# Router logits in four column strips out of one turned tile, with a wait ahead of a unit's transposes

## The chip, the cores and the metric

One core of a Trainium2 chip runs the whole program in one launch. The metric is the device time of that launch in microseconds (us), lower is better. The core has a matrix engine (TensorE, "PE"; its weight loads are the rows "PEld"), VectorE ("DVE"), ScalarE ("ACT"), GpSimd ("POOL") and SyncE ("SP"), which here only issues DMA transfers. Each engine takes its instructions in order and waits on semaphores of the others.

## The reference

The input x has 8 sequences of 2880 rows of 192 numbers, all float32. First a causal convolution: with weight (8 heads x 7 taps) turned by a softmax into seven shares per head, every row becomes the weighted sum of itself and the six rows before it, head by head (24 numbers a head).

The 23040 smoothed rows then go through a mixture of experts with two levels of choice:

```
g_logits = x @ w_group                      # 192 x 4
g_idx    = argmax(g_logits);  g_w = softmax(g_logits)[g_idx]
e_logits = x @ w_expert[g_idx]              # 192 x 4
e_idx    = argmax(e_logits);  e_w = softmax(e_logits)[e_idx]
out      = g_w * e_w * (relu(x @ w1[g_idx, e_idx]) @ w2[g_idx, e_idx])
```

w1 is 192 x 1024 and w2 1024 x 192 for each of 16 experts. Each row is worked on by one expert only.

## The kernel before, in words

**Routing.** The rows are cut into 192 blocks of 120, and the blocks into 18 units: the first six have 4, 8, 12, 8, 8 and 8 blocks, the other twelve 12. A unit is a Python generator, `unit` (line 397), whose `yield`s cut it into turns; `step` (line 1087) gives one turn to each of the two or three units alive, in a circle. A unit's turns are, in order: eight convolution turns (lines 437 to 456, one head each: a matmul with a band matrix and an eviction into the unit's tile `xc`, which has three buffers); the transposes of its smoothed rows, four blocks at a time ("a quarter"), columns 0 to 127 in `turn_a` and columns 128 to 191 in `turn_b`, two blocks' narrow columns side by side; the router's logits, `logits` and `logits_back`; softmax and choice on VectorE; the DMA of the smoothed rows to DRAM (`xcd`, line 569, issued by ScalarE); and the lists of rows for each expert, written to DRAM by an indirect DMA (line 644).

**The logits.** The router has 20 outputs, padded to 32 columns. `logits` puts the result of quarter q on partitions 32q to 32q + 31 of one PSUM bank. A quarter has 4 x 120 = 480 rows, so the matmul on the wide part is 480 columns long; the narrow part needs two more of 240 columns, one for the even and one for the odd blocks, with router weights that have zeros in the other half (`wrb`). A unit of 12 blocks thus fills three strips of 32 partitions, one of 8 blocks two, and one of 4 blocks one. ScalarE evicts the bank, `logits_back` transposes the result back so that rows lie on partitions, in four pieces, and ScalarE evicts again. The turned rows are in the tiles `ta` and `tb` with three buffers each, one for every quarter.

**Experts.** Each visit to an expert takes slots of 256 rows: the rows are gathered from `xcd` (line 716), turned (line 738), multiplied by w1 (`hidden`, line 808), evicted with ReLU by ScalarE and VectorE, multiplied by w2 (`back`, line 827), scaled and scattered to the output (line 887). Products are made of float32r pieces, a high and a low part of each operand, so weights are first split (line 674). Once all units are routed, slots are taken in pairs of 512 columns (`hidden_pair`, line 779); a pair's three operands come from `pair_room` (line 769): the high part from the tile `xa`, the low part from `lts`, and the narrow part from `ta`. At the end a tail of 18 smaller slots uses weights that the table `tab` names; every second one loads its weights into the then unused buffers `xin` and `xc` (line 654).

**What sets the order.** The first five units are routed by steps alone, then 100 more steps are taken, and then every expert slot advances the routing by a rate that spreads the remaining turns (line 1225). The program text gives each instruction a priority; a planner then orders each engine's instructions by priority and by costs it assumes, and gives out buffers of a pool as they come free. A few instructions are held in the order of the program. A unit of 12 blocks has 47 turns; from the ninth unit on, one starts when the unit before it has had 23.

Of the kernel before, what the change touches and what calls it, by code (L numbers as in the profile page):

```python
# [9 lines left out]
F32 = mybir.dt.float32  # L10
F32R = mybir.dt.float32r
BF16 = mybir.dt.bfloat16
F16 = mybir.dt.float16
I32 = mybir.dt.int32
U32 = mybir.dt.uint32
AF = mybir.ActivationFunctionType
# [4 lines left out]
P = 128  # L21
BT = 120
UB = 12
QB = 4
# [7 lines left out]
NTAB = 128  # L32
# [4 lines left out]
def conv_moe_kernel(  # L37
# [10 lines left out]
    nc = tc.nc  # L48
# [30 lines left out]
    NL = G + E  # L79
# [13 lines left out]
    for b in range(B):  # L93
        k = b * NB
# [78 lines left out]
    const = ctx.enter_context(tc.tile_pool(name="const", bufs=1))  # L173
    dram = ctx.enter_context(tc.tile_pool(name="dram", bufs=1, space=bass.MemoryType.DRAM))
    pa = ctx.enter_context(tc.tile_pool(name="pa", bufs=1))
    XCB = 2
    pa2 = ctx.enter_context(tc.tile_pool(name="pa2", bufs=XCB))
# [13 lines left out]
    XE = XW + D2  # L191
# [57 lines left out]
    NC = 32  # L249
    wr = const.tile([P, 2, NC], F32, name="wr")  # L250
    nc.vector.memset(wr, 0.0)
    wev = w_expert.rearrange("g d e -> d g e")
    for q, (p0, r0, n) in enumerate(((0, 0, P), (0, P, D2), (D2, P, D2))):
        c = min(q, 1)
# [4 lines left out]
    ident = const.tile([P, P], F32, name="ident")  # L259
# [8 lines left out]
    def clear_table():  # L268
# [12 lines left out]
        out=tri, in_=ones, pattern=[[1, P]], compare_op=ALU.is_gt, fill=0.0, base=0, channel_multiplier=-1,  # L281
# [12 lines left out]
    for nb in sorted({n for _, n in units}):  # L294
# [35 lines left out]
        out=sel, in_=ident.rearrange("p (e l) -> p e l", e=E), axis=AX.X, op=ALU.add)  # L330
    nc.gpsimd.iota(io[:, 0:1], pattern=[[0, 1]], base=0, channel_multiplier=1)
    nc.vector.tensor_scalar(
        out=io[:, 1:2], in0=io[:, 0:1], scalar1=LE - 1, scalar2=None, op0=ALU.bitwise_and)
# [6 lines left out]
    for g in range(NSK):  # L340
        nc.sync.dma_start(
            out=skew[0:R, g * HG:(g + 1) * HG],
            in_=bass.AP(wvd.tensor, wvd.offset + VL - KS - (BT - 1) + g * HG * VL, [[1, R], [VL, HG], [1, VW]]),
# [6 lines left out]
    for v in (3, 4):  # L350
        n = units[v][1]
# [12 lines left out]
    band = const.tile([P, H, BT], F32, name="band")  # L364
    for h in range(H):
        nc.scalar.activation(
            out=band[0:R, h], in_=skew[0:R, h, BT - 1::-1], func=AF.Exp, bias=wm[0:R, h:h + 1],
# [2 lines left out]


    QS = UB // QB
    wrb = const.tile([P, 2, NC], F32, name="wrb")

    def router_weights():
# [9 lines left out]
    for i in range(NXG):  # L385
        t = const.tile([P, XE + XW], F32, name=f"xg{i}")
# [10 lines left out]
    def unit(u, pre=None):  # L397
        c0, nb = units[u]
# [57 lines left out]
                nc.scalar.activation(out=xo, in_=pv, func=AF.Copy)  # L456
        nc.scalar.activation(out=xc[0:BT, 0:nb:2, XW:XE], in_=xc[0:BT, 1:nb:2, 1 + P:XW], func=AF.Copy)
        lg = rt.tile([P, UB, NL], F32, name="lg")[:, 0:nb]
        QN = QB * BT
        NQ = nb // QB  # L460
        parts = {}

        def turn_a(q):
            psa = bank("t")
            for i in range(QB):
                nc.tensor.transpose(psa[:, i * BT:(i + 1) * BT], xc[0:BT, q * QB + i, 1:1 + P], ident[0:BT, 0:BT])
            ta = pa.tile([P, 512], F32, name="ta", bufs=QS)[:, 0:QN]
            nc.scalar.activation(out=ta, in_=psa[:, 0:QN], func=AF.Copy)
            parts[q] = (ta,)

        def turn_b(q):
            psb = bank("t")
            tb = pa.tile([P, QN // 2], F32, name="tb", bufs=QS)
            for i in range(QB // 2):
                k = q * QB + 2 * i
                nc.tensor.transpose(psb[:, i * BT:(i + 1) * BT], xc[0:BT, k, 1 + P:XE], ident[0:BT, 0:BT])
            nc.scalar.activation(out=tb, in_=psb[:, 0:QN // 2], func=AF.Copy)
            parts[q] += (tb,)

        turned_logits = []  # L480

        def logits():
            lgp = bank("l")
            half = QB // 2
            for step in range(3):
                for q in range(NQ):
                    ta, tb = parts[q]
                    o = lgp[q * NC:(q + 1) * NC, 0:QN]
                    if step == 0:
                        nc.tensor.matmul(out=o, lhsT=wr[:, 0], rhs=ta, start=True, stop=False)  # L490
                    else:
                        j = step - 1
                        nc.tensor.matmul(
                            out=o.rearrange("p (i j t) -> p i j t", i=half, j=2)[:, :, j], lhsT=wrb[:, j],
                            rhs=tb.rearrange("p (i t) -> p i t", i=half), start=False, stop=j == 1)
            lgt = pa.tile([P, 512], F32, name="lts", bufs=2)
            nc.scalar.activation(out=lgt[0:NQ * NC, 0:QN], in_=lgp[0:NQ * NC, 0:QN], func=AF.Copy)
            turned_logits.append(lgt)

        def logits_back():  # L500
            lgt = turned_logits.pop()
            w = NQ * NC
            back = bank("l")
            for i in range(QB):
                nc.tensor.transpose(back[0:BT, i * w:(i + 1) * w], lgt[0:w, i * BT:(i + 1) * BT], ident[0:w, 0:w])
            nc.scalar.activation(
                out=lg[0:BT].rearrange("p (q i) n -> p i q n", i=QB),
                in_=back[0:BT, 0:QB * w].rearrange("p (i q n) -> p i q n", i=QB, n=NC)[:, :, :, 0:NL], func=AF.Copy)

        ga, gl, rest = gaps(u)  # L510
        events = {}
# [86 lines left out]
        for b0 in range(0, nb, HB2):  # L598
            n = min(HB2, nb - b0)
# [169 lines left out]
    def pair_room():  # L769
        hi = ff.tile([P, 2, SLOT], F32R, name="xa").rearrange("p a b -> p (a b)")  # L770
        lo = pa.tile([P, 512], F32, name="lts", bufs=2).bitcast(F32R)
        xb = pa.tile([P, 512], F32, name="ta", bufs=QS).bitcast(F32R)
        return hi, lo, xb

    def turn_half(X, k, xs):
# [153 lines left out]
    def table(first=None, nbig=NBIG, nsmall=NSMALL):  # L929
# [115 lines left out]
            return  # L1045
        nc.sync.dma_start(out=tabd, in_=enti)
        yield
        tabt = const.tile([1, NTAB, 4], I32, name="tab")
        nc.sync.dma_start(out=tabt, in_=tabd.unsqueeze(0))
        yield tabt  # L1050

# [434 lines left out]
```

## Time and profile before

| | us |
|---|---|
| median of 3 runs | 1137.57 |
| lowest and highest | 1131.44, 1137.88 |
| profiled execution | 1133.71 |
| its span in the trace | 1131.9 |

| engine | busy us | share of the span |
|---|---|---|
| TensorE, matmul | 1084.2 | 96% |
| TensorE, weight load | 971.6 | 86% |
| VectorE | 749.3 | 66% |
| ScalarE | 642.9 | 57% |
| GpSimd | 524.5 | 46% |

The profile is of one execution. Matmuls are pipelined, so the durations of neighbours overlap, and what one costs is read from the distance of the starts. The granted clock of TensorE (PEclk) is given as a share of 2.4 GHz. A name before the arrow is what an instruction writes, behind it what it reads; "pm", "ph" and "po" are pools of PSUM banks. Routing runs from the start to about 360 us, the first expert slots start at about 104 us, pairs run from about 445 to 972 us, and the tail to the end.

### The profile page before, as it was taken

The numbers are of one execution on the slowest core, as the hardware profiler recorded it, in microseconds if no ns is written. First come the engines' busy times: TensorE is split into PE (matmuls) and PEld (weight loads), VectorE is DVE, ScalarE is ACT, GpSimd is POOL, SyncE is SP. The second block draws the span as 40 slices with busy tenths as digits, with TensorE's granted clock in tenths as the row PEclk, the third lists the DMA queues.
The fourth block names the chain that finished last, engine by engine and source line by source line (L and its number), as shares of the span: only waits on it lengthen the run. The fifth ranks groups of instructions, "written<-read, shape, count | busy, mean of one in ns | idle before, by whom it ended". The sixth has DMA issues, their size and how long they took to land.

```text
span 1131.9 us, 21005 instructions
## 1 busy us (share of the span) xinstructions
PE 1084.2 (96%) x7148; PEld 971.6 (86%) x7148; DVE 749.3 (66%) x1671; ACT 642.9 (57%) x1362; POOL 524.5 (46%) x611
## 2 busy tenths in 40 slices
PE   6888999999999999999999999999999999999996
PEld 5555998888998998999999999989898889999995
DVE  4668988887777765566645655655555556687874
ACT  5465677666565455455545554554454555677883
POOL 3013234432333656545454545454525554487773
PEclk9889999999999999999999999999999999999998
DMA  8669799887644433233253322332223335399970
GB/s 221 184 189 245 202 247 232 243 220 194 179 128 131 136 113 94 76 101 112 54 163 102 113 73 78 101 114 69 80 87 108 107 93 160 118 257 262 257 207 20
DMA packets 143168, 166.08 MB, mean 147 GB/s; under 512 B 18946, under 2 KB 124397, under 8 KB 143054
## 3 DMA queue, kind: packets, MB, share of 16 engines
q1 hardware_dynamic: 100974, 111.04, 35.9%
q0 software_dynamic: 18752, 35.85, 10.2%
q10 hardware_dynamic: 23328, 17.80, 6.4%
q8 instruction: 57, 0.93, 0.4%
q14 instruction: 57, 0.47, 0.1%
HBM read 129.43 MB, written 36.58 MB: 147 GB/s over the span
## 4 chain that ended last, share of the span: by engine, by line
PE 75%; DVE 9%; ACT 6%; DMA 6%; issue 3%; POOL 0%; SPq 0%; POOLq 0%; ACTq 0%; DVEq 0%
PE ph L785 21%; PE ph L816 11%; PE pm L800 7%; PE po L800 7%; PE po L834 6%; PE pm L804 3%; PE po L804 3%; PE pm L447 3%; PE po L838 3%; DMA xcd<-xc 2%; DVE hl L822 1%; PE ph L851 1%; DMA rawc<-in_moe_w 1%; ACT ah L681 1%; DMA xg<-xcd,idpt 1%
## 5 line engine op out<-in xcount | busy, mean ns | idle before, releaser
L887 POOL DMA_INDIRECT out<-ys,idp x160 | 173.2, 1082 | 308.4 <-DVE ys L897 223.0
L790 DVE SCALAR_TENSOR_TENSOR hl<-ph,hh 128x512 fp32r<-128x512 f32 x208 | 141.9, 690 | 142.3 <-ACT hh L789 141.8
L789 ACT ACTIVATE hh<-ph 128x512 fp32r<-128x512 f32 x208 | 122.6, 599 | 164.8 <-PE ph L785 161.2
L716 POOL DMA_INDIRECT xg<-xcd,idp x160 | 177.4, 1109 | 75.9 <-PE ph L753 25.3
L834 PE MATMUL po<-cw,hh 128*128 128x384 f32 x592 | 190.0, 376 | 0.4 <-DVE ys L897 0.4
L816 PE MATMUL ph<-xa,ah 128*128 128x256 f32 x592 | 169.8, 308 | 1.6 <-DVE hl L822 1.6
L838 PE MATMUL po<-cw,hl 128*128 128x192 f32 x592 | 148.9, 252 | 0.0
L800 PE MATMUL pm<-cw,hh 128*128 128x384 f32 x416 | 134.1, 359 | 0.0
L800 PE MATMUL po<-cw,hh 128*128 128x384 f32 x416 | 133.9, 359 | 0.0
L822 DVE SCALAR_TENSOR_TENSOR hl<-ph,hh 128x512 fp32r<-128x512 f32 x148 | 100.7, 684 | 44.8 <-ACT hh L821 44.4
L821 ACT ACTIVATE hh<-ph 128x512 fp32r<-128x512 f32 x148 | 88.1, 597 | 65.8 <-PE ph L816 63.6
L816 PEld LDWEIGHTS ph<-xa,ah 128*128 128x128 f32 x592 | 113.0, 191 | 4.7 <-DVE hl L822 1.8
L834 PEld LDWEIGHTS po<-cw,hh 128*128 128x128 f32 x592 | 111.6, 189 | 5.3 <-issue 2.7
L838 PEld LDWEIGHTS po<-cw,hl 128*128 128x128 f32 x592 | 113.4, 192 | 1.8
L804 PE MATMUL pm<-cw,hl 128*128 128x192 f32 x416 | 104.2, 251 | 0.0
L804 PE MATMUL po<-cw,hl 128*128 128x192 f32 x416 | 104.0, 250 | 0.0
L785 PE MATMUL ph<-xa,ah 128*128 128x512 f32 x208 | 86.0, 414 | 4.7 <-DVE hl L822 4.7
L816 PE MATMUL ph<-xa,al 128*128 128x256 f32 x296 | 84.1, 284 | 0.0
L804 PEld LDWEIGHTS po<-cw,hl 128*128 128x128 f32 x416 | 79.1, 190 | 5.8
L816 PE MATMUL ph<-xb,bh 128*128 128x256 f32 x296 | 83.9, 283 | 0.0
L816 PE MATMUL ph<-xb,bl 128*128 128x256 f32 x296 | 83.9, 283 | 0.0
L785 PE MATMUL ph<-lts,ah 128*128 128x512 f32 x208 | 83.2, 400 | 0.0
(272 smaller groups left out, 2666.3 us busy)
## 6 DMA issues: line engine op xcount, KB each, us to landing
rawc<-in_moe_w SPq DMA_DIRECT2D x82, 384.0 KB
raw<-in_moe_w SPq DMA_DIRECT2D x41, 512.0 KB
raw<-in_moe_w SPq DMA_DIRECT2D x82, 256.0 KB
xcd<-xc ACTq DMA_DIRECT2D x13, 1085.6 KB
xin<-in_x SPq DMA_DIRECT2D x7, 1134.0 KB
xc<-in_moe_w SPq DMA_DIRECT2D x18, 384.0 KB
xin<-in_x SPq DMA_DIRECT2D x6, 1039.5 KB
xin<-in_moe_w SPq DMA_DIRECT2D x9, 512.0 KB
```

What stands on the lines that cost most here:

```text
L716: nc.gpsimd.indirect_dma_start(out=xs[t][:, 0:XW], out_offset=None, in_=xcd[0:known, :], in_offset=bass.IndirectOffsetOnAxis(ap=ids[:, t, ...
L785: nc.tensor.matmul(out=hp.rearrange("p a b -> p (a b)"), lhsT=W[wgt][:, fs], rhs=xx, start=i == 0, stop=i == len(ops) - 1)
L789: nc.scalar.activation(out=hh, in_=hp, func=AF.Relu)
L790: nc.vector.scalar_tensor_tensor(out=hl, in0=hp, scalar=0.0, in1=hh.bitcast(F32), op0=ALU.max, op1=ALU.subtract,)
L800: nc.tensor.matmul(out=oo[t][:, 0:2 * D], lhsT=hh[:, ts], rhs=cw[:, f].rearrange("p a d -> p (a d)"), start=f == 0, stop=False,)
L804: nc.tensor.matmul(out=oo[t][:, 0:D], lhsT=hl[:, ts], rhs=cw[:, f, 0, :], start=False, stop=f == NF - 1,)
L816: nc.tensor.matmul(out=hp[:, j], lhsT=wgt[:, fs], rhs=xx, start=i == 0, stop=i == len(ops) - 1)
L821: nc.scalar.activation(out=hh, in_=hp, func=AF.Relu)
L822: nc.vector.scalar_tensor_tensor(out=hl, in0=hp, scalar=0.0, in1=hh.bitcast(F32), op0=ALU.max, op1=ALU.subtract,)
L834: nc.tensor.matmul(out=oo[t][:, 0:2 * D], lhsT=hh[:, j, ts], rhs=cw[:, f].rearrange("p a d -> p (a d)"), start=f == 0, stop=False,)
L838: nc.tensor.matmul(out=oo[t][:, 0:D], lhsT=hl[:, j, ts], rhs=cw[:, f, 0, :], start=False, stop=f == NF - 1,)
L887: nc.gpsimd.indirect_dma_start(out=outviews[nscat[0] % len(outviews) if view is None else view], out_offset=bass.IndirectOffsetOnAxis(ap=i ...
```

## The change

The turned rows of a unit now lie in one constant tile, `tall`, with four quarter slots, and `tbll` for the narrow part. A unit takes as many neighbouring slots as it has quarters. Ahead of its transposes it yields turns until the logits of every unit that had these slots before are in the program (`read`, `quads`). A strip is no longer a quarter but the position g of a block within its quarter: strip g reads block g of every quarter, 120 columns from each, by a strided operand. There are always four strips, of 120 columns times the number of quarters, and two rounds of matmuls instead of three, since a strip has only even or only odd blocks and needs one of the two narrow weights. The way back takes one full transpose for each quarter, 128 partitions in and 128 columns out, instead of four narrower ones. Two things move: the narrow operand of a pair takes a buffer of `xc` instead of `ta`, and the tail's table takes the place of the convolution's band matrix instead of a tile of its own.

```diff
     QS = UB // QB
+    QRING = 4
+    tall = const.tile([P, QRING, QB, BT], F32, name="ta")
+    tbll = const.tile([P, QRING, QB // 2, BT], F32, name="tb")
+    quads = [-1] * QRING
+    read = {-1}
...
-        QN = QB * BT
         NQ = nb // QB
-        parts = {}
+        HQ = QB // 2
+        k = min(range(QRING - NQ, -1, -1), key=lambda k: max(quads[k:k + NQ]))
+        while any(v not in read for v in quads[k:k + NQ]):
+            yield
+        quads[k:k + NQ] = [u] * NQ
+        ta, tb = tall[:, k:k + NQ], tbll[:, k:k + NQ]
...
-            ta = pa.tile([P, 512], F32, name="ta", bufs=QS)[:, 0:QN]
-            nc.scalar.activation(out=ta, in_=psa[:, 0:QN], func=AF.Copy)
-            parts[q] = (ta,)
+            nc.scalar.activation(
+                out=ta[:, q], in_=psa[:, 0:QB * BT].rearrange("p (i t) -> p i t", i=QB), func=AF.Copy)
...
-            for step in range(3):
-                for q in range(NQ):
-                    ta, tb = parts[q]
-                    o = lgp[q * NC:(q + 1) * NC, 0:QN]
+            for step in range(2):
+                for g in range(QB):
+                    o = lgp[g * NC:(g + 1) * NC, 0:NQ * BT].rearrange("p (q t) -> p q t", q=NQ)
                     if step == 0:
-                        nc.tensor.matmul(out=o, lhsT=wr[:, 0], rhs=ta, start=True, stop=False)
+                        nc.tensor.matmul(out=o, lhsT=wr[:, 0], rhs=ta[:, :, g], start=True, stop=False)
                     else:
-                        j = step - 1
-                        nc.tensor.matmul(
-                            out=o.rearrange("p (i j t) -> p i j t", i=half, j=2)[:, :, j], lhsT=wrb[:, j],
-                            rhs=tb.rearrange("p (i t) -> p i t", i=half), start=False, stop=j == 1)
+                        nc.tensor.matmul(out=o, lhsT=wrb[:, g % 2], rhs=tb[:, :, g // 2], start=False, stop=True)
+            read.add(u)
             lgt = pa.tile([P, 512], F32, name="lts", bufs=2)
-            nc.scalar.activation(out=lgt[0:NQ * NC, 0:QN], in_=lgp[0:NQ * NC, 0:QN], func=AF.Copy)
+            nc.scalar.activation(out=lgt[:, 0:NQ * BT], in_=lgp[:, 0:NQ * BT], func=AF.Copy)
...
-            for i in range(QB):
-                nc.tensor.transpose(back[0:BT, i * w:(i + 1) * w], lgt[0:w, i * BT:(i + 1) * BT], ident[0:w, 0:w])
+            for q in range(NQ):
+                nc.tensor.transpose(back[0:BT, q * P:(q + 1) * P], lgt[:, q * BT:(q + 1) * BT], ident)
...
-        xb = pa.tile([P, 512], F32, name="ta", bufs=QS).bitcast(F32R)
+        xb = pa2.tile([P, UB, XE], F32, name="xc", bufs=3).rearrange("p b d -> p (b d)")[:, 0:512].bitcast(F32R)
...
-        tabt = const.tile([1, NTAB, 4], I32, name="tab")
+        tabt = band.rearrange("p h t -> p (h t)").bitcast(I32)[0:1, 0:NTAB * 4].rearrange("p (j c) -> p j c", c=4)
```

## Rows read from the trace of the kernel before

**Rows 1.** The page: busy time of TensorE, and the chain's shares by engine.
```profile
PE 1084.2 (96%) x7148; PEld 971.6 (86%) x7148; DVE 749.3 (66%) x1671; ACT 642.9 (57%) x1362; POOL 524.5 (46%) x611
...
PE 75%; DVE 9%; ACT 6%; DMA 6%; issue 3%; POOL 0%; SPq 0%; POOLq 0%; ACTq 0%; DVEq 0%
```

**Rows 2.** Stretches: from:to, length; PE, PEld, DVE, ACT, POOL busy us; PEclk, DMA share, GB/s.
```profile
0.00:105.00 105.00, 84.98 (x475) 56.00 (x475) 61.99 (x258) 58.16 (x160) 24.45 (x46) 0.92 0.76 210
105.00:360.00 255.00, 249.28 (x1947) 225.42 (x1946) 210.99 (x515) 169.02 (x361) 89.61 (x77) 0.99 0.78 202
...
445.00:972.00 527.00, 522.26 (x3059) 471.77 (x3058) 305.87 (x609) 260.58 (x551) 259.38 (x371) 1.00 0.33 99
```

**Rows 3.** Chain that ended last, 0 to 106 us: start us, us, what.
```profile
34.68 0.94 PE ph L490 x6
...
60.85 0.92 PE po L490 x2
...
62.89 0.33 PE po L490
63.22 0.20 PE po L493
63.42 0.20 PE po L490
63.62 1.01 PE po L493 x5
64.66 0.57 ACT lts L497
...
70.53 7.36 DMA xcd<-xc
...
87.32 13.28 DMA xcd<-xc
```

**Rows 4.** Stretches, instructions of line 490 alone: PE and PEld busy, PEclk, DMA share, GB/s.
```profile
0.00:105.00 105.00, 12.12 (x36) 1.82 (x36) 0.92 0.76 210
105.00:360.00 255.00, 10.06 (x60) 1.51 (x60) 0.99 0.78 202
```

**Rows 5.** The same of line 493 alone.
```profile
0.00:105.00 105.00, 12.46 (x72) 4.57 (x72) 0.92 0.76 210
```

**Rows 6.** Timeline of TensorE around one unit's logits: start us, us, what, operand sizes, count.
```profile
358.08 1.01 PE L490 MATMUL pm<-ta,wr 128*32 128x480 f32 x6
358.91 0.99 PE L493 MATMUL pm<-tb,wrb 128*32 128x240 f32 x12
359.82 0.44 PE L834 MATMUL po<-cw,hh 128*128 128x384 f32 x1
...
361.47 0.49 PE L505 MATMUL pm<-ident,lts 96*120 96x96 f32 x4
361.74 0.36 PE L816 MATMUL ph<-xa,ah 128*128 128x256 f32 x1
```

**Rows 7.** Timelines of SyncE, ScalarE and TensorE: a spare load, and between two pairs.
```profile
575.74 0.98 SPq L669 DMA_DIRECT2D xc<-in_moe_w  x2
...
953.43 0.27 ACT L761 ACTIVATE ta<-ph 64x128 fp32r<-64x128 f32 x1 [0.81 <-DVE lts L755]
...
953.91 0.40 PE L785 MATMUL ph<-ta,bl 128*128 128x512 f32 x1
...
955.98 0.39 PE L785 MATMUL ph<-ta,bh 128*128 128x512 f32 x1
```

**Rows 8.** Stretches of 2 us around 46 to 58 us, columns as in rows 2.
```profile
44.00:46.00 2.00, 0.59 (x2) 0.28 (x2) 0.35 (x1) 1.20 (x5) 0.00 (x0) 0.96 0.00 0
46.00:48.00 2.00, 1.71 (x8) 1.56 (x8) 1.86 (x6) 1.56 (x7) 0.00 (x0) 0.50 0.00 0
...
56.00:58.00 2.00, 2.00 (x13) 1.88 (x12) 0.86 (x7) 0.55 (x3) 0.00 (x0) 0.50 0.26 70
```

**Rows 9.** Waits of ScalarE, 60 to 112 us: us in total, times, longest.
```profile
ACT xc L456 <- DMA xcd<-xc: 9.6, 3, 3.8
```

More of the change, by code (lines that the diff above doesn't have):

```diff
@@ L466, in turn_a @@
                 nc.tensor.transpose(psa[:, i * BT:(i + 1) * BT], xc[0:BT, q * QB + i, 1:1 + P], ident[0:BT, 0:BT])
-            ta = pa.tile([P, 512], F32, name="ta", bufs=QS)[:, 0:QN]
-            nc.scalar.activation(out=ta, in_=psa[:, 0:QN], func=AF.Copy)
-            parts[q] = (ta,)
+            nc.scalar.activation(
+                out=ta[:, q], in_=psa[:, 0:QB * BT].rearrange("p (i t) -> p i t", i=QB), func=AF.Copy)
         def turn_b(q):
             psb = bank("t")
-            tb = pa.tile([P, QN // 2], F32, name="tb", bufs=QS)
-            for i in range(QB // 2):
+            for i in range(HQ):
                 k = q * QB + 2 * i
                 nc.tensor.transpose(psb[:, i * BT:(i + 1) * BT], xc[0:BT, k, 1 + P:XE], ident[0:BT, 0:BT])
-            nc.scalar.activation(out=tb, in_=psb[:, 0:QN // 2], func=AF.Copy)
-            parts[q] += (tb,)
+            nc.scalar.activation(
+                out=tb[:, q], in_=psb[:, 0:HQ * BT].rearrange("p (i t) -> p i t", i=HQ), func=AF.Copy)
         turned_logits = []
@@ L483, in logits @@
             lgp = bank("l")
-            half = QB // 2
-            for step in range(3):
-                for q in range(NQ):
-                    ta, tb = parts[q]
-                    o = lgp[q * NC:(q + 1) * NC, 0:QN]
+            for step in range(2):
+                for g in range(QB):
+                    o = lgp[g * NC:(g + 1) * NC, 0:NQ * BT].rearrange("p (q t) -> p q t", q=NQ)
                     if step == 0:
-                        nc.tensor.matmul(out=o, lhsT=wr[:, 0], rhs=ta, start=True, stop=False)
+                        nc.tensor.matmul(out=o, lhsT=wr[:, 0], rhs=ta[:, :, g], start=True, stop=False)
                     else:
-                        j = step - 1
-                        nc.tensor.matmul(
-                            out=o.rearrange("p (i j t) -> p i j t", i=half, j=2)[:, :, j], lhsT=wrb[:, j],
-                            rhs=tb.rearrange("p (i t) -> p i t", i=half), start=False, stop=j == 1)
+                        nc.tensor.matmul(out=o, lhsT=wrb[:, g % 2], rhs=tb[:, :, g // 2], start=False, stop=True)
+            read.add(u)
             lgt = pa.tile([P, 512], F32, name="lts", bufs=2)
-            nc.scalar.activation(out=lgt[0:NQ * NC, 0:QN], in_=lgp[0:NQ * NC, 0:QN], func=AF.Copy)
+            nc.scalar.activation(out=lgt[:, 0:NQ * BT], in_=lgp[:, 0:NQ * BT], func=AF.Copy)
             turned_logits.append(lgt)
@@ L501, in logits_back @@
             lgt = turned_logits.pop()
-            w = NQ * NC
             back = bank("l")
-            for i in range(QB):
-                nc.tensor.transpose(back[0:BT, i * w:(i + 1) * w], lgt[0:w, i * BT:(i + 1) * BT], ident[0:w, 0:w])
+            for q in range(NQ):
+                nc.tensor.transpose(back[0:BT, q * P:(q + 1) * P], lgt[:, q * BT:(q + 1) * BT], ident)
             nc.scalar.activation(
-                out=lg[0:BT].rearrange("p (q i) n -> p i q n", i=QB),
-                in_=back[0:BT, 0:QB * w].rearrange("p (i q n) -> p i q n", i=QB, n=NC)[:, :, :, 0:NL], func=AF.Copy)
+                out=lg[0:BT], in_=back[0:BT, 0:nb * NC].rearrange("p (b n) -> p b n", n=NC)[:, :, 0:NL], func=AF.Copy)
         ga, gl, rest = gaps(u)
```

## The prediction, made before the change was run

> **What bounds the kernel now.** I read the page first, then the same numbers by stretch, then the chain of waits in the first 105 us, then single instructions. The page has TensorE busy for 96% of the span and on 75% of the chain that ended last [rows 1]: whatever takes time off TensorE can shorten the run, if it is taken where TensorE is not waiting. The stretches tell where that is [rows 2]. From 105 to 360 us, where routing and experts share the core, TensorE is busy 249.28 of 255 us; from 445 to 972 us, experts alone, 522.26 of 527 us, and there the change takes nothing from it. In the first 105 us it is busy only 84.98 us, and the chain there [rows 3] leaves TensorE for two long transfers of the smoothed rows to DRAM: 7.36 us from 70.53 and 13.28 us from 87.32. The chain of the first expert goes through both, to 100.60. So a microsecond of TensorE is worth a microsecond after 105 us, and something between nothing and a microsecond before.
>
> **The logits, 105 to 360 us.** This stretch holds 60 instructions of line 490 [rows 4], which is ten units of 12 blocks, six each: a matmul is two instructions and there are three strips. One unit in full [rows 6]: strips 480 wide from 358.08 to 358.91, the two rounds 240 wide from 358.91 to 359.82, together 1.74 us for 480 + 240 + 240 = 960 columns. That strips really lie side by side is seen on the chain [rows 3]: one strip of the fifth unit took 0.92 us (two instructions), three strips of the third unit 0.94 us (six). So the cost goes by columns per strip, not by strips. After the change there are two rounds of four strips, each 3 x 120 = 360 wide: 720 columns, at 1.74/960 = 1.81 ns a column 1.305 us. That is 0.435 us less for a unit and 4.35 us for ten. A fourth strip is in no row; the bounds are 0.435 us less (four cost as three) and, if the fourth ran by itself behind the other three, 1440 columns or 2.61 us, 0.87 us more. I take the first, as one and three differ by 0.02 us.
>
> The way back: four transposes of 96 columns from 361.47 to 361.74 [rows 6], 0.07 us each; afterwards three of 128, 0.09 us each by columns. 0.27 us both times: nothing. The eviction of the logits (0.57 us for 480 columns [rows 3]) gets a quarter shorter on ScalarE, which is busy 169.02 of 255 us here [rows 2] and not the bound: nothing, 0.1 us a unit if it were.
>
> Does all of the 4.35 us arrive? TensorE idles 5.7 us in this stretch, so some of its waits are for others and only get longer. I take 3.5 us; ends 0 and 4.35.
>
> **The logits, before 105 us.** Eight units lie here. In the fifth, five pieces stand on the chain with other work between them: 0.92 + 0.33 + 0.20 + 0.20 + 1.01 = 2.66 us [rows 3], because a strip ran as soon as its own tile was turned, while another unit's work filled in; the eviction started only at 64.66, 3.8 us after the first strip. After the change no strip can start before all rows of the unit are turned, and then all four go together: 2 x 240 = 480 columns, 0.87 us. That is 1.8 us less work and up to 2.9 us earlier, before the transfer at 70.53 is issued. For all eight units lines 490 and 493 were busy 12.12 + 12.46 = 24.6 us [rows 4, 5]; one unit of 4 blocks, four of 8 and three of 12 make 240 + 4 x 480 + 3 x 720 = 4320 columns, 7.8 us at 1.81 ns. The upper end is therefore 16.8 us less, too high since pieces overlap each other and their neighbours; the lower end is 0, if the two transfers and the evictions behind them stay where they are. Nearest is what stood ahead of the first of them: 1.8 us for the fifth unit, and 1.3 us for the first, which falls from 960 columns to 240. I take 2.7 of these 3.1 us, the rest going into waits for VectorE.
>
> **The wait put in.** Four quarter slots serve all units: a unit of 12 blocks needs three of them, so its transposes are put into the program only after the logits of every unit whose slots it takes. Following the turns of the units in the code (units counted from 0), unit 2 waits 2 turns, unit 3 seven, unit 6 one, unit 7 six; from unit 8 on none, since a unit starts 23 turns behind the one before it, which has its logits out by then. What queues behind is, on ScalarE, the unit's evictions of the turned rows and then the next unit's evictions of its convolution; on TensorE, convolutions that need their banks; VectorE waits with the softmax. In the kernel before, three tiles for each half gave nearly the same wait, at the eviction instead. Lower end 0, upper end 16 turns at the pace of 105 to 360 us (ten units of 47 turns in 255 us, 0.54 us): 8.7 us later for the first expert. The wait that is already there is nearest, so I take 0.5 us.
>
> **The moved buffer.** The third operand of an expert pair (the narrow part of the turned rows) leaves the three "ta" tiles for the three "xc" buffers. Those also hold spare weights for the tail: the first such load is issued at 575.74 us [rows 7] and keeps its buffer until the tail begins, at about 970 us. Two are left, as many as the other two operands have. In front of the tail a second spare load wants one; then a pair's evictions wait for the last reader of the pair before. That reader starts at 953.91, the next pair's first reader at 955.98; between lie 2.07 us, less its own 0.40 us, for four small evictions on each engine, 0.27 us each on ScalarE: 1.1 us in 1.7, so it nearly fits. I take 0.5 us once; ends 0, and 1.5 us for each of the 26 pairs that the plan of slots has, 39 us. The table in the place of the band is one small load, long after the last convolution: nothing, 0.3 us if it had to wait.
>
> **Sum.** -3.5 - 2.7 + 0.5 + 0.5 = -5.2 us. The profiled execution took 1133.71 us (span 1131.9), 3.9 below the median shown; the four times shown have a mean of 1135.2. From that mean, 1130.0.
>
> **A rule against it.** TensorE was busy 0.59 of the 2 us from 44, and from 46 to 58 us, six rows of 2 us, the granted clock was 0.50, the lower of its two levels [rows 8]. Shorter logits leave longer holes in just this part. The Trainium skill, "TensorE: Matmul & The Clock Gate" (Part 1), says that the clock is throttled by default and only sustained matmul work releases it, an idle spell bringing the half rate back. The trace agrees in these rows. By the trace's sum alone the time is 1130; by the page's rule the early gain would be paid back.
>
> **Rivals.**
> 1. *The early gain comes through* (0.20). For it: ScalarE stood 9.6 us behind such transfers between 60 and 112 us [rows 9], and an earlier fifth unit moves the whole row of them. Then two thirds of 16.8, and 4.35, less 1 for the waits, 14.5 us: 1121.
> 2. *The clock gives it back* (0.12). Another spell like that from 46 us, some 10 us of matmuls at half speed, costs 5 us: 1135. Against: work that waits moves into the holes.
> 3. *ScalarE parks behind one more transfer* (0.10), the slower side. From 80 to 105 us ScalarE takes its evictions in order; if the shifted turns put a convolution's eviction, whose buffer waits for a DRAM write, ahead of the first expert's rows once more, the price is a transfer like the long one, 13.28 us: 1143, and up to 1150 with the upper end of the wait. It decides once it exceeds the 6 us gained. Against: it already stands so once.
> 4. *Four strips are not four at once* (0.05): 0.87 us more a unit instead of 0.435 less, 13 us over ten, and the early units gain little: 1145.
> 5. *Pairs wait for the moved buffer* (0.03): up to 39 us, 1165; it needs two spare loads held from early on.
>
> The forecast itself has 0.50, within 1123 to 1137.
>
> **Numbers.** One per cent of the median, 11.4 us, is about what a measurement here tells from no change: under 1126.2 is faster, over 1148.9 slower. Faster: rival 1 and 0.08 of the forecast's lower part, 0.28. Slower: half of rivals 3 and 4 and all of 5, 0.10. Same: 0.62. The range leaves out the far ends of rivals 1, 3 and 4 and all of 5: 1119 to 1144.
>
> **What would show it.** Eight instructions a unit on each of the two logits lines (six and twelve before), and some 1.3 us from the first strip to the next work around 350 us; near 1.7 us or more would say rival 4. The chain's second long transfer ending before 100 us shows the early gain, after 105 us rival 3. More rows at 0.50 before 100 us show rival 2. TensorE at 99% through the pairs shows the moved buffer harmless. I am wrong if the logits get shorter and the first expert still starts later.

## The result and the profile after

The changed kernel takes 1148.91 us (median of 4 runs, 1146.87 to 1152.01) where the kernel before takes 1135.17 beside it: a ratio of 1.0126, 95% interval 1.0083 to 1.0169. It is 13.7 us slower, where 5.2 us faster was forecast. The profiled span grew from 1131.9 to 1147.8 us.

The page of the changed kernel, against [rows 1]: TensorE is busy 11.3 us less and the span is 15.9 us longer, so it idles 27 us more.

```profile
PE 1072.9 (93%) x7124; PEld 967.1 (84%) x7124; DVE 751.6 (65%) x1671; ACT 642.8 (56%) x1362; POOL 523.5 (46%) x611
...
PE 70%; DVE 6%; DMA 5%; issue 4%; ACT 3%; POOL 1%; POOLq 0%; DVEq 0%; ACTq 0%; SPq 0%
```

The stretches of [rows 2] in the changed kernel (same columns). TensorE's busy time falls from 84.98 to 67.30 us before 105 us and from 249.28 to 241.93 after: more than the logits give back, so work was pushed out of these stretches.

```profile
0.00:105.00 105.00, 67.30 (x427) 48.45 (x427) 59.03 (x242) 53.21 (x149) 22.33 (x44) 0.88 0.76 190
105.00:360.00 255.00, 241.93 (x1865) 217.16 (x1864) 203.88 (x499) 163.92 (x347) 87.19 (x74) 0.97 0.82 203
445.00:972.00 527.00, 518.37 (x3048) 467.99 (x3048) 305.00 (x607) 258.92 (x548) 265.70 (x383) 1.00 0.35 101
```

Landmarks of both traces (starts, us) say where the 15.9 us arise. A slot's start is its first product with w1.

| | before | after | difference |
|---|---|---|---|
| first expert slot | 102.9 | 113.3 | +10.4 |
| twelfth slot | 269.5 | 281.4 | +11.9 |
| last slot before the pairs | 430.8 | 442.8 | +12.0 |
| first pair | 442.8 | 456.1 | +13.3 |
| last pair | 955.3 | 970.7 | +15.4 |
| end | 1131.9 | 1147.8 | +15.9 |

Two thirds are there at the first slot. The pairs add 2.1 us, all in the step to the last one (21.6 us for 19.1).

**The logits are shorter, as forecast.** The line of the wide part alone, then that of the narrow part (columns: stretch, length, PE and PEld busy, PEclk, DMA share, GB/s), against [rows 4, 5]: 80 instructions in ten units are eight for each.

```profile
105.00:360.00 255.00, 8.12 (x80) 1.57 (x80) 0.97 0.82 203
...
105.00:360.00 255.00, 7.88 (x80) 2.60 (x80) 0.97 0.82 203
```

TensorE's timeline around one unit, against [rows 6]: four strips from 353.35, four from 353.98, the next work at 354.70. That is 1.35 us instead of 1.74; 1.305 was forecast. Four strips run side by side.

```profile
353.35 0.81 PE L495 MATMUL pm<-ta,wr 128*32 128x360 f32 x8
353.98 0.79 PE L497 MATMUL pm<-tb,wrb 128*32 128x360 f32 x8
354.70 0.46 PE L633 MATMUL pm<-ohv,ohl 120*128 120x32 f16 x12
```

**The transposes of unit 3 come late.** In the kernel before, its wide transposes start at 33.2 us. Here one block's transpose stands at 38.41 (one of four for the quarter) and the others follow after a hole of 6.74 us. TensorE's timeline, before and then after:

```profile
33.21 0.98 PE L466 MATMUL pm<-ident,xc 120*128 120x120 f32 x8
```

```profile
37.91 0.66 PE L633 MATMUL pm<-ohv,ohl 120*128 120x192 f16 x6 [0.58 <-DVE ohv L619]
38.41 0.27 PE L475 MATMUL pm<-ident,xc 120*128 120x120 f32 x1
45.41 0.48 PE L633 MATMUL pm<-ohv,ohl 120*128 120x192 f16 x2 [6.74 <-DVE ohv L619]
45.69 0.81 PE L475 MATMUL pm<-ident,xc 120*128 120x120 f32 x3
```

The hole begins at VectorE, which TensorE waits for. VectorE itself waits 6.81 us until an earlier list of rows, issued to DRAM at 35.56, has landed, since that write reads the small tile `rowi`, which VectorE is to fill anew. In the kernel before that list was issued at 32.03, and the same step ran at 38.04 without such a wait (a second profile of it has 2.2 us there). The wait comes without the waits of the change as well: strips_by_quarter and ring_no_turns, described below, have it with 5.6 and 6.5 us, but there the transposes of unit 3 stand ahead of it.

```profile
44.67 0.16 DVE L626 TENSOR_TENSOR rowi<-rows,goff 128x1 int32<-128x1 f32 x1 [6.81 <-DMA idtab<-lsi,rowi]
```

Then ScalarE's timeline, before and after. Unit 3's logits are out of PSUM at 58.65 (47.28 before), the transfer of its rows is issued at 63.49 (57.51 before), and the next eviction of a convolution stands 6.46 us behind a transfer. The list of unit 4, which the first expert needs, is issued at 87.7 us (77.2 before), and the first expert's rows are fetched from 95.3 us (87.1 before).

```profile
44.80 0.33 ACT L456 ACTIVATE xc<-ph 120x192 f32<-120x192 f32 x1 [6.80 <-issue]
...
47.28 0.29 ACT L506 ACTIVATE lg<-pm 120x160 f32<-120x160 f32 x1
```

```profile
44.08 0.33 ACT L461 ACTIVATE xc<-ph 120x192 f32<-120x192 f32 x1 [6.28 <-DMA xcd<-xc]
...
58.65 0.30 ACT L508 ACTIVATE lg<-pm 120x160 f32<-120x160 f32 x1 [4.17 <-PE pm L507]
...
63.49 0.32 ACTq L570 DMA_DIRECT2D xcd<-xc  x1
...
71.95 0.42 ACT L461 ACTIVATE xc<-ph 120x288 f32<-120x288 f32 x1 [6.46 <-DMA xcd<-xc]
```

ScalarE's waits up to 115 us: the wait for the transfers of smoothed rows, in the changed kernel and then in the kernel before (us in total, times, longest). This looks like one wait more and 7.3 us more, but it is not shown to be. An eviction into `xc` waits near 44 us in both kernels: 6.28 us in the changed one, put down to the transfer, and 6.80 us in the kernel before, put down to "issue" (6.73 us in a second profile of that kernel, put down to TensorE). With it counted, the sums are 20.6 and 20.1 us: the waits come later, and are not longer in total.

```profile
ACT xc L461 <- DMA xcd<-xc: 20.6, 5, 6.5
```

```profile
ACT xc L456 <- DMA xcd<-xc: 13.3, 4, 3.8
```

**The last pair.** In the changed kernel's trace SyncE issues the tail's second spare load into `xc` at 960.51. ScalarE then evicts the last pair's narrow operand at 967.97, just after the pair before has read it for the last time (967.03, 0.40 long), and the second half only behind a split of weights. TensorE waits 1.39 us and starts at 970.70. Of the 21.60 us of this step it is busy 20.21 with 117 matmuls, where the kernel before is busy for all of its 19.10 with 113: of the 2.5 us, 1.4 are idle time, and the rest is work that now stands ahead of the last pair. SyncE, ScalarE and TensorE:

```profile
960.51 0.96 SPq L670 DMA_DIRECT2D xc<-in_moe_w  x2
```

```profile
967.00 1.06 ACT L682 ACTIVATE ah<-xin 128x1024 fp32r<-128x1024 f32 x1 [1.50 <-PE ph L786]
967.97 0.41 ACT L762 ACTIVATE xc<-ph 64x128 fp32r<-64x128 f32 x2
968.28 0.58 ACT L790 ACTIVATE hh<-ph 128x512 fp32r<-128x512 f32 x1
968.76 1.05 ACT L690 ACTIVATE bh<-xin 128x1024 fp32r<-128x1024 f32 x1
969.83 0.44 ACT L762 ACTIVATE xc<-ph 64x128 fp32r<-64x128 f32 x2
```

```profile
967.03 0.40 PE L786 MATMUL ph<-xc,bl 128*128 128x512 f32 x1
...
970.70 0.47 PE L786 MATMUL ph<-xa,ah 128*128 128x512 f32 x1 [1.39 <-DVE hl L791]
```

### The profile page after: what moved, and what is told of

It is laid out like the page before. It is cut to its first block, busy times and chain, and to the rows that moved or that the text cites. A ratio compares the mean times of both kernels' runs of the same rounds, so it can differ in the third digit from the quotient of the medians.

```text
span 1147.8 us, 20939 instructions
## 1 busy us (share of the span) xinstructions
PE 1072.9 (93%) x7124; PEld 967.1 (84%) x7124; DVE 751.6 (65%) x1671; ACT 642.8 (56%) x1362; POOL 523.5 (46%) x611
## 4 chain that ended last, share of the span: by engine, by line
PE 70%; DVE 6%; DMA 5%; issue 4%; ACT 3%; POOL 1%; POOLq 0%; DVEq 0%; ACTq 0%; SPq 0%
PE ph L786 21%; PE ph L817 11%; PE pm L801 7%; PE po L801 7%; PE po L835 6%; PE pm L805 3%; PE po L805 3%; PE pm L452 3%; PE po L839 3%; DMA xg<-xcd,idpt 2%; DMA rawc<-in_moe_w 1%; DVE hl L823 1%; DMA raw<-in_moe_w 1%; PE ph L852 1%; DVE cw L698 1%
## 5 line engine op out<-in xcount | busy, mean ns | idle before, releaser
L698 DVE TENSOR_TENSOR cw<-rawc,cw 128x768 fp32r<-128x768 f32 x82 | 75.9, 954 | 15.3 <-ACT cw L697 14.8
L786 PE MATMUL ph<-xc,bh 128*128 128x512 f32 x208 | 82.4, 396 | 1.3 <-DVE xc L763 1.3
```

The costliest lines, as they stand in the source:

```text
L786: nc.tensor.matmul(out=hp.rearrange("p a b -> p (a b)"), lhsT=W[wgt][:, fs], rhs=xx, start=i == 0, stop=i == len(ops) - 1)
```

## The experiments

Sixteen runs in four sets, each set beside its own runs of the kernel before: 1136.09, 1145.91, 1148.07 and 1138.10 us. A ratio holds within its set only. The ratios and 95% intervals are the recorded ones; they are not exactly the quotients of the medians shown. The second and the fourth set were taken on a chip of the same number, although their kernels before differ by 7.8 us.

### First set: the parts one by one (before: 1136.09 us)

**waits_only**: the kernel before with the turns given away, and nothing else.

```diff
+    QRING = 4
+    quads = [-1] * QRING
+    read = {-1}
...
+        k = min(range(QRING - NQ, -1, -1), key=lambda k: max(quads[k:k + NQ]))
+        while any(v not in read for v in quads[k:k + NQ]):
+            yield
+        quads[k:k + NQ] = [u] * NQ
...
+            read.add(u)
```

> The kernel before, with nothing of the change but the turns that units 2, 3, 6 and 7 give away (2, 7, 1, 6); logits, tiles and buffers as before. Theory 1, the turns put in cost the time (unit 3's wide transposes fall behind the 7 us hole at 38 to 45 us and the first expert comes 8 to 10 us later): 1143 to 1148, first expert slot after 109 us. Theory 2, the turns are harmless and what costs is that no strip may start before its whole unit is turned: 1133 to 1138, first slot at 102 to 105 us.

Measured: 1149.82 us, 1.0141 (1.0097 to 1.0186). The first slot starts at 114.1 us. This is theory 1, a little above its 1143 to 1148 us. The waits alone cost as much as the whole change did beside its own kernel before (1.0126).

**strips_by_quarter**: the kernel before with four strips, read quarter by quarter (120 columns a matmul) out of the old tiles; no ring, no waits, no moved buffer.

```diff
+            for q in range(NQ):
+                ta, tb = parts[q]
+                for step in range(2):
+                    for g in range(QB):
+                        o = lgp[g * NC:(g + 1) * NC, q * BT:(q + 1) * BT]
```

> The kernel before, with four strips of 32 columns and two rounds, but a tile for each quarter as before, so matmuls of 120 columns for each quarter and strip; no ring, no turns given away, no buffer moved. Theory 1 (the turns cost the time, shorter logits are a gain): 1127 to 1132, a unit's logits near 350 us in about 1.3 us instead of 1.74. Theory 2 (the joint start costs): also below before, since quarters start by themselves. If short matmuls eat the gain or four strips do not lie side by side: 1135 or more, with logits of 1.7 us or longer.

Measured: 1136.80 us, 1.0011 (0.9987 to 1.0035). A unit's logits take 1.37 us here, so they are shorter, and the shorter logits give nothing that can be measured; both theories had expected a gain. The first slot starts later all the same, at 109.6 us, and ScalarE stands at the first expert's rows:

```profile
ACT xa L751 <- PE pm L748: 8.3, 1, 8.3
```

**ring_no_turns**: the changed kernel, with units 1, 3, 5 and 7 turned into a weight buffer that is idle then, so that no unit waits.

```diff
+        if u in (1, 3, 5, 7):
+            if not lent:
+                lent.append(wsp.tile([P, NF, 2, D], F32R, name="cw").bitcast(F32).rearrange("p f a d -> p (f a d)"))
```

> The changed kernel, but units 1, 3, 5 and 7 lay their turned rows into a weight buffer that is idle at that time, so that no unit gives a turn away; joint strips and moved buffers stay. Theory 1: 1132 to 1139 (the 8 to 10 us come back), first slot at 102 to 106 us. Theory 2: 1146 to 1150, first slot after 110 us.

Measured: 1146.63 us, 1.0104 (1.0069 to 1.0140). By the ratios only 2.5 us of the change come back, so the costs don't simply add. These are the numbers that were expected for theory 2, the joint start of the strips (1146 to 1150 us, first slot after 110; it starts at 110.3). The third set speaks against it as the whole cause: neither_again has the joint start too and is 1.0024. Whether the borrowed weight buffer costs something itself was not tested. Against strips_by_quarter the profile shows the step to the last pair at 21.5 us instead of 19.1, and a tail of 180.4 us instead of 177.0; the rest of the 9.8 us between their medians is in no row that I can name. One tail says little: the two profiles of the kernel before have 176.6 and 178.0 us.

**pairs_keep_room**: the changed kernel, the pairs' narrow operands three to one `xc` buffer that is held through all pairs.

```diff
-        xb = pa2.tile([P, UB, XE], F32, name="xc", bufs=3)...
+        k = nroom[0] % 3
+        nroom[0] += 1
+        xb = kept[0][:, k * 512:(k + 1) * 512]
```

> The changed kernel, but the pairs' narrow operand rotates inside one buffer of xc that is held through all pairs, so a spare load cannot take its place. If the moved buffer costs what the last pair shows (its start 15.4 us behind the kernel before, the pair ahead of it 12.9 us): 1145 to 1147, 2 to 3 us below the change. If that 2.5 us is something else: 1148 to 1150.

Measured: 1148.39 us, 1.0139 (1.0096 to 1.0182). The step to the last pair is back at 19.0 us, but the tail takes 179.4 us (177.1 in the changed kernel), and the ratio is no lower than the change's. That the moved buffer costs the whole any time is not shown by this run.

### Second set: where the waits cost (before: 1145.91 us)

**turns_behind**: the kernel before with the same numbers of turns, but behind the logits.

```diff
+        rest += {2: 2, 3: 7, 6: 1, 7: 6}.get(u, 0)
```

> The kernel before with the same 2, 7, 1 and 6 turns given away by units 2, 3, 6 and 7, but behind their logits (ahead of the lists) instead of ahead of the transposes. Theory 1a, it is the holding back of unit 3's transposes: back to 1134 to 1139, first slot before 108 us. Theory 1b, any turn that shifts the other units against each other costs it: 1146 to 1151, first slot after 110 us.

Measured: 1145.07 us, 0.9996 (0.9974 to 1.0017). Behind the logits the turns cost nothing in this set. The sixteen turns ahead of the transposes were not run beside it, only the two parts that follow.

**unit3_waits** and **units67_wait**: waits_only, with the wait for unit 3 alone, and for units 6 and 7 alone.

```diff
-        while any(v not in read for v in quads[k:k + NQ]):
+        while u in (3,) and any(v not in read for v in quads[k:k + NQ]):
```

> The kernel before with unit 3's turns alone given away ahead of its transposes. If unit 3 behind the hole at 38 to 45 us is the cause: 1144 to 1150, unit 3's logits back on rows after 57 us, first slot after 109 us. If it is the later units' turns or their number: 1135 to 1139.

> The kernel before with the turns of units 6 and 7 alone given away ahead of their transposes. If unit 3 is the cause: 1135 to 1139. If the lag of the routing behind its planned pace is (the last unit's list at 440 us instead of 378, pairs 1.3 us later, portions later): 1140 to 1148, with the last list after 400 us.

Measured: 1147.97 us, 1.0017 (0.9992 to 1.0043), and 1151.60 us, 1.0055 (1.0025 to 1.0086). For units 6 and 7 the interval lies clear above that of turns_behind, so their place ahead of the transposes does cost here. For unit 3 no cost is shown, though its first slot starts at 119.9 us and its logits are evicted at 63.6.

The turns are not those of the expectations: with the other units' waits gone the programs' order shifts, and unit 3 alone gives away five turns, units 6 and 7 alone two and seven. This holds in the fourth set too.

**no_turns_own_room**: ring_no_turns, with the pairs' narrow operands in the room of the ring tile, which is idle then.

> The changed kernel with no turn given away (odd early units in a borrowed buffer) and the pairs' narrow operand in the room of the turned rows instead of a buffer of xc. If the moved buffer costs what the pairs and the tail show there (2 us in the last pair, 3.8 us in the tail): 1139 to 1143. If not: 1145 to 1148.

Measured: 1149.69 us, 1.0029 (1.0009 to 1.0049); the step to the last pair is 19.1 us. The expected times rest on a kernel before of about 1136 us and can't be held against this set's 1145.91; by the ratio the lower expectation holds (1139 to 1143 beside 1136 would be 1.003 to 1.006).

### Third set: waits and buffer, two by two (before: 1148.07 us)

**change_again** and **no_turns_again** repeat the changed kernel and ring_no_turns; **turns_own_room** is the changed kernel with the operands in the ring's room, **neither_again** repeats no_turns_own_room.

> The changed kernel as it is, beside the three below, because chips differ by up to a per cent in the kernel before: its ratio is the one the others are held against. All theories: 1.008 to 1.017 of the kernel before.

> No turn given away, buffers moved as in the change (the same kernel as ring_no_turns). If the turns cost half a per cent or more here: at least 0.5% below change_again. If turns and moved buffers overlap: within 0.4% of it.

> The changed kernel with its turns, but the pairs' narrow operand in the room of the turned rows instead of a buffer of xc. If the moved buffer costs what the last pair and the tail show (2 to 6 us): 0.2 to 0.5% below change_again. If not: equal to it.

> No turns and own room (the same kernel as no_turns_own_room). Both costs gone, joint strips left: 1.000 to 1.004 of the kernel before, and below it (0.996) only if the shorter logits come through. If 0.8% or more stays, the joint start of the strips is the cause.

Measured: 1153.76 us, 1.0058 (1.0035 to 1.0081); 1154.36 us, 1.0054 (1.0021 to 1.0087); 1154.84 us, 1.0045 (1.0022 to 1.0067); and 1151.38 us, 1.0024 (1.0001 to 1.0046). Where the kernel before itself takes 1148 us, the whole change costs 6 us, less than the 1.008 expected of it. Taking the waits away gives back 0.04% here with the moved buffer and 0.21% without it, where half a per cent was the sign that they cost. The four intervals overlap, and even the order is not shown: by the medians turns_own_room is the slowest of the four. The step to the last pair is clean in every trace: 21.7 us with the moved buffer, 19.1 us without, in both pairs.

### Fourth set: the waiting units on one chip (before: 1138.10 us)

> The kernel before, unchanged, run as if it were a change: what two times of one program differ by here. Both theories expect 0.998 to 1.002. Its profile is a second execution of the kernel before: by the theory that unit 3's place decides the early loss, unit 3's logits are evicted near 47 us again and the first expert's slot starts near 103 us; by the rival that the first execution was a lucky one, the first slot starts at 108 us or later.

> The kernel before with the turns given away by units 2, 3, 6 and 7 and nothing else. If the turns have a price of their own, 1.010 to 1.014 as in the first run; if that first run owed it to its chip, 1.002 to 1.006.

> The kernel before with the seven turns of unit 3 alone. If unit 3's place behind the wait for the lists of rows is the early loss, most of what all the waits cost here: at least 6 us where they cost 12, first slot at 112 us or later. If the places of units 6 and 7 cost it, under 2 us.

> The kernel before with the turns of units 6 and 7 alone. If unit 3 is the loss, under 3 us and a first slot near that of the kernel before. If units 6 and 7 are, 6 us or more, between the first slot and the last slot before the pairs.

Measured, with landmarks of the profiles (us):

| | median | ratio | unit 3's logits evicted | first slot | unit 7's logits evicted | fifth slot | last before pairs | span |
|---|---|---|---|---|---|---|---|---|
| before_twin | 1136.09 | 0.9991 (0.9967–1.0016) | 50.2 | 105.8 | 103.9 | 165.1 | 435.7 | 1138.1 |
| unit3_waits_again | 1143.85 | 1.0059 (1.0037–1.0082) | 59.1 | 114.6 | 110.5 | 169.5 | 437.2 | 1142.7 |
| units67_wait_again | 1149.84 | 1.0119 (1.0066–1.0173) | 50.5 | 110.1 | 112.0 | 175.7 | 442.5 | 1144.3 |
| waits_only_again | 1150.60 | 1.0112 (1.0059–1.0165) | 60.7 | 116.2 | 118.1 | 173.9 | 447.1 | 1150.4 |

The kernel before has its first slot at 105.8 us in this second profile, between the 103 and the 108 us of the two expectations. My theory had unit 3 carry the loss. It makes the first slot 8.8 us later, but 7.3 of these are recovered by the last slot before the pairs. Another 3.1 us come after it, most of them between the first two pairs (23.2 us for 19.4). Units 6 and 7 are worth more: their wait costs 4.3 us at the first slot, 10.6 at the fifth, and 6.8 are still there at the last one before the pairs. Both together are no dearer in the medians than units 6 and 7 alone, whose profiled execution (1146.16 us) is the shortest of its four. The two stretches 20 to 100 and 100 to 165 us in the four profiles (columns as in [rows 2]), before_twin first, then unit 3, units 6 and 7, all:

```profile
20.00:100.00 80.00, 68.32 (x401) 43.37 (x401) 50.52 (x198) 45.70 (x122) 13.98 (x13) 0.91 0.74 203
100.00:165.00 65.00, 61.19 (x457) 54.34 (x457) 56.81 (x150) 42.69 (x94) 19.67 (x17) 0.97 0.82 224
```

```profile
20.00:100.00 80.00, 63.71 (x354) 42.20 (x352) 48.35 (x185) 42.75 (x113) 6.88 (x7) 0.85 0.75 195
100.00:165.00 65.00, 62.72 (x477) 53.45 (x476) 55.22 (x155) 40.60 (x88) 23.56 (x19) 0.97 0.81 214
```

```profile
20.00:100.00 80.00, 64.22 (x366) 40.97 (x365) 49.54 (x194) 42.44 (x112) 13.63 (x12) 0.89 0.73 198
100.00:165.00 65.00, 55.88 (x398) 46.65 (x397) 48.01 (x129) 36.55 (x77) 16.93 (x14) 0.95 0.74 202
```

```profile
20.00:100.00 80.00, 61.53 (x358) 40.63 (x356) 49.40 (x191) 40.91 (x111) 11.35 (x10) 0.87 0.70 186
100.00:165.00 65.00, 54.86 (x415) 47.86 (x416) 50.39 (x136) 38.19 (x81) 18.17 (x16) 0.95 0.74 202
```

TensorE's busy time over both stretches is 129.5, 126.4, 120.1 and 116.4 us: 3.1, 9.4 and 13.1 us less by 165 us, against 4.6, 6.2 and 12.3 us on the spans. (Busy time is not quite work: from 20 to 100 us the granted clock is 0.91, 0.85, 0.89 and 0.87.) With unit 3's wait the loss of busy time ends at 100 us; with that of units 6 and 7 it goes on while the experts already run. What TensorE waits for from 115 to 165 us in units67_wait_again is VectorE, at the lists of rows (`lsi`) and at the scaled outputs (`ys`); before_twin has no wait in that stretch. These waits don't tell the dear kernels from the cheap one, though: turns_behind, which lost nothing in its set, has 6.4 us of waits for VectorE in the same stretch (2.9 at `lsi`, 1.3 at `ys`, 2.2 at the low part of the hidden values).

```profile
PE po L842 <- DVE ys L905: 3.0, 3, 1.4
PE pm L450 <- DVE lsi L649: 1.9, 1, 1.9
PE pm L483 <- DVE lsi L649: 1.7, 1, 1.7
```

ScalarE's waits for the rows' transfers up to 115 us are 12.7 us in 4 in before_twin, 12.8 in 3 with unit 3's wait, 16.2 in 4 with that of units 6 and 7, and 30.2 in 5 with all. With the wait near 46 us counted, which stands under TensorE in before_twin (6.7 us) and under "issue" with units 6 and 7 (7.4 us), they are 19.4, 12.8, 23.6 and 30.2 us.

## Why the prediction was wrong

**The step that failed is "The wait put in".** I took 0.5 us because "the wait that is already there is nearest", with an upper end of 8.7 us for 16 turns at 0.54 us. The waits alone cost 13.7 us and, in the fourth set, 12.5. Two things were wrong with that step. The three old tiles make an *eviction* wait while the transposes are already in their place; the new wait moves the transposes themselves. And a turn has no fixed price: turns_behind has all sixteen, and in its set they cost nothing. I read it so that what counts is what stands between the old and the new place; that is argued and not shown. For unit 3 a hole stands there, 6.74 us in the changed kernel, but its logits are 9 us late in unit3_waits_again too, where the hole is 3.1 us and the turns are five. For units 6 and 7 it is the start of the experts, but turns_behind has nearly the same waits for VectorE without a loss.

Beside kernels before of 1136 and 1138 us, the waits are enough to cost what the change cost; that they are its whole cause is not shown. Taking them away from the changed kernel gave back 2.5 us by the ratios of the first set and the result, and 0.04 and 0.21% in the third set. Their price differs by set as well: 0.17% and 0.59% for unit 3, 0.55% and 1.19% for units 6 and 7, the smaller ones where the kernel before was slower.

**"The logits, before 105 us"**: -2.7 us was taken, and none came. With strips alone the first slot starts at 109.6 us in its profile (102.9 and 105.8 in the two of the kernel before). It is no accident of one run: the four profiles with the new logits and no waits in ring_no_turns, no_turns_again, no_turns_own_room and neither_again have 109.3 to 110.3 us. So 4 to 7 of the 10.4 us that the changed kernel's first slot is late come without any wait, and the sign that I gave this term at the first slot was wrong. In strips_by_quarter the logits of unit 6 are indeed evicted earlier (91.1 us, 95.3 in before_twin), but ScalarE then stands 8.3 us at the first expert's rows. None of this costs the whole, by the median: the first slot does not decide the time. The lower end that I gave, 0, is where the median lies.

**"The logits, 105 to 360 us"**: 0.39 us a unit against 0.435 forecast. That it arrives is not shown. From the twelfth to the nineteenth slot, with four units in it, the two profiles of the kernel before take 100.2 us and strips_by_quarter and ring_no_turns 98.6: 1.6 us, four times 0.4. But the same program as ring_no_turns takes 106.9 us there in the third set, and no_turns_own_room and neither_again 104.2 and 104.7, while kernels with the old logits range from 99.2 (units67_wait_again) to 102.6 (turns_behind). For the six units before that nothing shows: the fifth to the twelfth slot take 107.6 and 109.4 us in the kernel before, 109.0 with strips alone, 110.9 in the changed kernel, whose DMA share is 0.97 from 172 to 282 us:

```profile
172.00:282.00 110.00, 103.03 (x793) 93.47 (x793) 91.23 (x214) 72.34 (x154) 37.31 (x32) 0.97 0.97 233
```

I took such a stretch as bound by TensorE from its 249.28 of 255 us; that weights set its pace would fit, but no run took weights away there. Of the -3.5 us, the interval of strips_by_quarter (from 0.9987) leaves room for 1.5 at the most.

**"The moved buffer"**: 0.5 us was taken; the step to the last pair grows by 2.5, in every trace with it (21.5 to 21.7 us for 19.0 to 19.1), of which 1.4 us are idle time of TensorE. In the time of the whole it is not shown: pairs_keep_room got the step back and no time. The mechanism is the one forecast, at the place forecast: a spare load holds a buffer and the last pair's eviction waits for the last reader. What the 0.5 left out is what ScalarE had queued: two weight splits of 1.06 and 1.05 us go between, and the four small evictions no longer fit. Nothing of the 39 us of rival 5 came.

**One part was left out.** The turns given away are not counted in the plan that spreads the routing over the slots; the last list of rows is written at 439.6 us instead of 377.5, and the step from the last slot to the first pair takes 13.3 us instead of 12.0. The late list alone does not cost this: turns_behind writes it at 436.8 us, takes 12.0 us for the step and lost nothing in its set. A kernel that counts the turns was not run.

**The rivals.** Rival 3, the slower side, has the first expert later, as it happened, but its price was one long transfer more, and the changed kernel shows none: 20.6 us of such waits against 20.1, with the wait near 44 us counted in both. Rival 2 is there too: of the 39 stretches of 2 us from 36 to 114 us, those with a granted clock under 0.70 are 11 and 7 in the two profiles of the kernel before and 15 in the changed one. Without any wait they range from 11 in no_turns_again to 17 in strips_by_quarter and 18 in ring_no_turns, which is the same program as no_turns_again, so the count does not tell what they cost. It shows in small in strips_by_quarter: TensorE is busy 1.05 and 1.07 us of two stretches of 2 us, in the next one the granted clock is 0.52, near the lower level, and the step there takes 14.0 us instead of 12.6 in before_twin, which has the same two waits, 2.2 us together, and stays at 1.00. These 1.4 us undo a gain of the size of the logits':

```profile
376.00:378.00 2.00, 1.05 (x13) 0.94 (x13) 1.97 (x5) 0.60 (x1) 1.62 (x1) 1.00 0.82 207
378.00:380.00 2.00, 1.07 (x7) 0.91 (x7) 2.00 (x5) 0.00 (x0) 1.04 (x1) 1.00 0.81 202
380.00:382.00 2.00, 1.71 (x13) 1.71 (x13) 1.13 (x4) 0.00 (x0) 0.00 (x0) 0.52 0.56 182
382.00:384.00 2.00, 2.00 (x12) 2.00 (x11) 0.12 (x1) 0.76 (x2) 1.22 (x2) 0.62 0.00 0
```

Rival 4 fell with 1.35 us a unit, rival 1 with the first slot. Two of the rivals' sums were off: 39 us on 1130 are about 1169 and not 1165, and rival 3 with the upper end of the wait is 1151 or 1152 and not 1150.

**The sum by the runs**: strips +0.7 (1136.80 to 1136.09, not told from nothing), waits +13.7, buffer +1.4 by TensorE's idle time, together 15.8 where the change measured 13.7 beside another kernel before; with -6.2, +0.5 and +0.5 I had 5.2 us the other way. The condition I gave for being wrong, shorter logits and a later first expert, is what the trace shows; strips_by_quarter shows it too, without a loss.

**What stays open.** Why ring_no_turns, without any wait, is still 1.0104 in the first set, and why the same change costs 1.26% beside a kernel before of 1135 us and 0.58% beside one of 1148, and the waits less too. No profile of the kernel before was kept from the first three sets, so landmarks of their kernels can't be compared within the set. No version ran faster than the kernel before.

## What to carry to other kernels

When a resource is made scarcer, ask what is held up by it: an eviction that waits leaves the work ahead of it in its place, and a producer that waits moves; the number of turns does not tell the price. Sixteen of them ahead of the transposes cost 1.1 to 1.4% in two sets, and behind the logits nothing in another. Test a wait alone first: one run of the kernel before with nothing but the wait showed a loss as large as the whole. Then take it out of the changed kernel too: what did not come back there is still without a cause. A landmark is not the time: the first slot was 4 to 7 us late in strips_by_quarter, which lost nothing. And before two sums of waits are compared, look for the same wait under another name.

## What the runs showed of the hardware that I had not expected

The kernel before moved by 13 us between sets (1135.17 to 1148.07 us) while the changed one moved by 5 (1148.91 to 1153.76); no run here tells why, and two sets on a chip of the same number differ too (1145.91 and 1138.10 us). A write of a list by an indirect DMA, 1 us to issue, took 7.79 us to land at 125.57 us in the changed kernel, with VectorE's next list step behind it for 2.4 us, at a DMA share of 0.95. The one issued at 35.56 us held VectorE for 6.81 us, at a DMA share of 1.01:

```profile
125.57 7.79 DMA idtab<-lsi,rowi
...
133.46 0.16 DVE rowi L626
```
